# A one-core layer-norm MLP: one transpose group moved, two engines' halves swapped, and the bias turned on another engine

## The chip, the cores and the metric

The kernel runs on one core of a Trainium2 chip. The core has five engines with instruction streams of their own: TensorE (PE in the profile; its weight loads are listed apart as PEld), VectorE (DVE), ScalarE (ACT), GpSimd (POOL) and SyncE (SP). They meet only through semaphores. Transfers between the chip's main memory and the core's own memory are issued by SP and, for the first two of them, by ACT. The metric is the device time of one execution in microseconds (us); lower is better.

## What is computed

```python
def _layernorm(x, axis=-1, eps=1e-5):
    m = jnp.mean(x, axis=axis, keepdims=True)
    v = jnp.var(x, axis=axis, keepdims=True)
    return (x - m) / jnp.sqrt(v + eps)

def reference(x, w1, b1, w2, b2):
    y = _layernorm(x, axis=-1)
    h = _gelu(jnp.einsum("bsd,df->bsf", y, w1) + b1)
    return jnp.einsum("bsf,fd->bsd", h, w2) + b2
```

All arrays are bf16: x is 2048 x 1024, w1 is 1024 x 3584, b1 has 3584 elements, w2 is 3584 x 1024, b2 has 1024. The GELU is the tanh form.

## The kernel before

The 2048 rows of x are 16 tiles of 128 rows, in 4 blocks of 4 tiles. A block is normalised, transposed (so that the 1024 features lie on partitions, 8 slices of 128), multiplied by w1 in 28 output rows of 128 features x 512 columns (8 matmuls each), passed through the GELU with b1 as a bias per partition, and multiplied by w2 in 8 groups of 28 matmuls; DVE adds b2 and SP stores the result. All of w1 and w2 stays in the core's memory.

The program is written as five lists of operations, one for each engine, in the order in which each engine will run them (`_Prog`, `_emit`): an operation names the events that it waits for, and an engine that waits holds all that is queued behind. The order of TensorE is written out by hand for block 0. DVE's later order (scalings of block 0, normalisation and transposes of the next blocks, additions of b2) is merged by estimated times at the end of the function.

Block 0 is the part that the change touches.

- *Loads.* ACT's queue issues the second half of tile 0 (`x0b`, columns 512 to 1023) and then tile 1 (`x1`). SP's queue issues the rest in the order of `SP_FIRST_LOADS`: the first half of tile 0 (`x0a`), six rows of w1 for the first 7 output rows (`w0` to `w5`), the two halves of tile 2, the bias `b1`, two more rows of w1, the halves of tile 3, then wide chunks of w1 (`w8` and on), later blocks of x, and w2. Every transfer is line 190.
- *The head.* Tile 0 is not waited for in full. DVE takes statistics of `x0b` (`op_stats(0, 1)`, line 261) while ACT sums `x0a` with an accumulating copy (line 495, result `half_sb`). DVE joins the two into the row's mean times 4 (`op_mean0`, line 272, event `m4`), and writes tile 0 centred, but not scaled, into `o_sb` in two pieces (line 278): columns 0 to 255, then 256 to 1023. Tile 1 is centred in the same way, in place (line 283). Tiles 2 and 3 are normalised in full (line 287), with 1/sqrt(variance) from POOL (line 265). The missing scale of tiles 0 and 1 is applied by DVE to the sums in PSUM (line 426), after `ops_rbc` has spread the row scales over partitions with 16 small transposes (lines 322 and 330).
- *Transposes of block 0* are TensorE's (`pe_T`, line 376), each group followed by a copy by ACT out of PSUM (line 383). Tile 0 has three groups of slices, 0 to 1, 2 to 4 and 5 to 7 (`GROUPS_0`); the first and the third go to the bank `ps_t`, the second to another. Tiles 1 to 3 have two groups of four, all in `ps_t`; a group waits until ACT has read out the one before it in its bank. Groups are put between the small matmuls (128 columns, line 416) at the indices in `T_PUTS`, counted in the matmuls of block 0's first 7 rows; the first two groups of tile 0 precede them all. Tile 0's third group stands behind 14 matmuls, tile 1's two groups behind 21 and 35.
- *The bias* is loaded as 28 rows of 128 (`b1r_sb`) and transposed by one small TensorE matmul ahead of tile 2's second group (`B1_AT`, line 368) into the free end of that group's bank; a second ACT copy makes the 128 x 28 tile `b1_sb` (line 387), which every GELU (line 433) reads.
- *Warm-up.* 34 matmuls on constants run from the start (line 491), 3 more wait for `m4`, and 3 stand behind the second transpose group.
- *After the first 7 rows* come rows 7 to 27 of block 0 with 512-column matmuls, each waiting for a free PSUM bank: row 7 takes `ps_t`, row 8 the bank of row 0, which its GELU must have read.
- *Constants.* POOL writes `ones`, the identity, `nhalf` and two constant fields of `st_sb` (lines 257 and 258); DVE waits for the last (line 499) before anything else.

Of the kernel before, what the change touches and what calls it, by code (L numbers as in the profile page):

```python
# [20 lines left out]
WARM_A = ((34, None), (3, "m4"))  # L21
WARM_B = 3
N_CENTRED = 2
T_PUTS = {0: (None, None, 14), 1: (21, 35), 2: (96, 118), 3: (140, 156)}
NORM = {0: (0, 2, 8), 1: (0, 4, 8), 2: (0, 4, 8)}
GROUPS_0 = (0, 2, 5, 8)
WAVE_ROWS_0 = 6
WAVE_K = (0, 2, 4, 5, 6, 8)
B1_AT = (2, 1)
GROUPS_1 = (0, 4, 8)  # L30
W1_CHUNK_COLS = (512, 512, 1024, 640)
N_W2_CHUNKS = 4
SP_FIRST_LOADS = ("x0a", "w0", "w1", "w2", "w3", "w4", "w5", "x2a", "x2b", "b1", "w6", "w7", "x3a", "x3b", "w8")
ACT_FIRST_LOADS = ("x0b", "x1")

T_PE_START = 5.7
# [55 lines left out]
def bass_standalone__mixer_channel_mlp__prompt_kernel(  # L92
# [10 lines left out]
    ST, D = xf.shape  # L103
    F = w1.shape[1]
    NT = ST // P
    DT = D // P
    FT = F // P
# [3 lines left out]
    HC = D // 2  # L111
# [34 lines left out]
    with ExitStack() as es:  # L146
# [5 lines left out]
        x_sb = sb("x_sb", [P, NT, D], BF16)  # L152
# [1 line left out]
        hT_sb = sb("hT_sb", [P, FT, TB], BF16)  # L154
        o_sb = sb("o_sb", [P, NOB, D], BF16)
        b2_sb = sb("b2_sb", [P, D], BF16)
        b1r_sb = sb("b1r_sb", [FT, P], BF16)
        b1_sb = sb("b1_sb", [P, FT], F32)
        ident = sb("ident", [P, P], BF16)
        ones = sb("ones", [P, P], BF16)  # L160
# [25 lines left out]
        x_ev = {}  # L186
        w1_issued = set()

        def dma(dst, src, sig, nbytes):
            dma_q[0].op(lambda e, dst=dst, src=src: e.dma_start(dst, src), sig=sig, sem="d_" + sig, inc=16)  # L190
            dma_bytes[0] += nbytes
            est[sig] = DMA_T0 + dma_bytes[0] / DMA_BYTES_PER_US

# [19 lines left out]
        def issue(item):  # L213
            if item[0] == "x" and item[-1] in "ab":
                i, h = int(item[1:-1]), "ab".index(item[-1])
                dma(x_sb[:, i, h * HC:(h + 1) * HC], xf[i * P:(i + 1) * P, h * HC:(h + 1) * HC], f"x{i}_{h}",
                    P * HC * 2)
                x_ev[i] = (f"x{i}_0", f"x{i}_1")
            elif item == "b1":
                dma(b1r_sb[:, :], b1.rearrange("(t p) -> t p", p=P), "b1", F * 2)  # L220
            elif item[0] == "x":
                load_x_tile(int(item[1:]))
            elif item[0] == "w" and int(item[1:]) < len(w1_chunks):
                load_w1(int(item[1:]))
# [7 lines left out]
        for i in range(TPB):  # L232
            if i not in x_ev:
                load_x_tile(i)
            else:
                for h, evn in enumerate(x_ev[i]):
                    if evn not in est:
                        issue(f"x{i}" + "ab"[h])
        if "b1" not in est:
            issue("b1")  # L240
        for ci in range(len(w1_chunks)):
            if ci not in w1_issued:
# [14 lines left out]
        pool.op(lambda e: e.memset(st_sb[:, :, 12:14], 0.0))  # L257
        pool.op(lambda e: e.memset(st_sb[:, :, 14:15], LN_EPS * D), sig="eps")

        def op_stats(i, h):  # L260
            return (lambda e, i=i, h=h: e.bn_stats(st_sb[:, i, 6 * h:6 * (h + 1)], x_sb[:, i, h * HC:(h + 1) * HC]),  # L261
                    [x_ev[i][h]], f"st{i}_{h}", 0.65)
# [6 lines left out]
                    [f"st{i}_0", f"st{i}_1", "eps"], f"mv{i}", 0.33)  # L269

        def op_mean0():
            return (lambda e: e.tensor_scalar(out=m4_sb[:, :], in0=st_sb[:, 0, 7:8], scalar1=st_sb[:, 0, 10:11],  # L272
                                              scalar2=half_sb[:, :], op0=ALU.add, op1=ALU.add),
                    ["st0_1", "half"], "m4", 0.1)

        def op_norm(i, c0, c1, sig):
            if i == 0:
# [16 lines left out]
        def ops_norm(i):  # L294
            cuts = NORM.get(i, (0, DT))
            y_ev[i] = []
            res = []
            for k, (j0, j1) in enumerate(zip(cuts[:-1], cuts[1:])):
                res.append(op_norm(i, j0 * P, j1 * P, f"y{i}_{k}"))
                y_ev[i] += [f"y{i}_{k}"] * (j1 - j0)  # L300
            return res

        def ln_seq(tiles, between):
            seq = []
            prev = None
            for i in tiles:
                for h in range(2):
                    seq.append(op_stats(i, h))
                    if h == 0 and prev is not None:
                        seq += ops_norm(prev)  # L310
                        prev = None
                seq.append(op_aggr(i))
                if i + 1 in between:
                    prev = i
                else:
                    seq += ops_norm(i)
            return seq

        def ops_rbc():
            res = []  # L320
            for i in range(N_CENTRED):
                res.append((lambda e, i=i: e.tensor_scalar(out=rq_sb[:, i, :], in0=ones[:, 0:32],
                                                           scalar1=rstd_sb[:, i:i + 1], scalar2=(1.0 if i else 0.25),
                                                           op0=ALU.mult, op1=ALU.mult),
                            ["ones", f"rstd{i}"], f"rq{i}", 0.1))
            for tq in range(4):
                for q in range(4):
                    src = rq_sb[32 * tq:32 * (tq + 1), :, :]
                    dst = rbc_sb[32 * q:32 * (q + 1), :, 32 * tq:32 * (tq + 1)]
                    res.append((lambda e, src=src, dst=dst: e.transpose(out=dst, in_=src), [f"rq{N_CENTRED - 1}"],  # L330
                                ("rbc" if tq == 3 and q == 3 else None), 0.1))
            return res
# [27 lines left out]
        def pe_T(i, groups, k, with_b1=False):  # L360
            blk, t = divmod(i, TPB)
            j0, j1 = groups[k], groups[k + 1]
            bname, bap = t_banks[k if i == 0 else 0]
            evs = yT_ev.setdefault(i, [None] * DT)
            if with_b1:
                o = (j1 - j0) * P
                b1t = bap[:, o:o + FT]
                pe.op(lambda e: e.transpose(out=b1t, in_=b1r_sb[:, :], identity=ident[0:FT, 0:FT]),  # L368
                      waits=["ident", "b1"] + ([bank_read[bname]] if bname in bank_read else []))
            for j in range(j0, j1):  # L370
                waits = []
                if j == j0:
                    waits = ["ident"] + ([bank_read[bname]] if bname in bank_read else [])
                if j == j0 or y_ev[i][j] != y_ev[i][j - 1]:
                    waits.append(y_ev[i][j])
                pe.op(lambda e, i=i, j=j, o=(j - j0) * P, bap=bap: e.transpose(  # L376
                    out=bap[:, o:o + P], in_=(x_sb[:, i] if i else o_sb[:, 0])[:, j * P:(j + 1) * P],
                    identity=ident[:, :]),
                    waits=waits, sig=(f"tp{i}_{k}" if j == j1 - 1 else None))
# [3 lines left out]
            act.op(lambda e, dst=dst, src=src: e.copy(out=dst, in_=src), waits=[f"tp{i}_{k}"], sig=f"te{i}_{k}")  # L383
            bank_read[bname] = f"te{i}_{k}"
            if with_b1:
                bank_read[bname] = "b1c"
                act.op(lambda e: e.copy(out=b1_sb[:, :], in_=b1t), waits=[f"tp{i}_{k}"], sig="b1c")
            pe_t[0] += (j1 - j0) * 0.056

        crit = []  # L390
# [98 lines left out]
        def warm(n, gate=None):  # L489
            for _ in range(n):  # L490
# [4 lines left out]
        act.op(lambda e: e.activation(out=o_sb[:, 1, 0:HC], in_=x_sb[:, 0, 0:HC], func=ACT.Copy, scale=2.0 / HC,  # L495
                                      accum_out=half_sb[:, :]), waits=[x_ev[0][0]], sig="half")
        for n, gate in WARM_A:
            warm(n, gate)
        dve.op(None, waits=["eps"])
        head = [op_stats(0, 1), op_mean0()] + ops_norm(0) + ln_seq([1], ()) + [op_stats(0, 0), op_aggr(0)]  # L500
        for o in head + ln_seq(list(range(2, TPB)), ()) + ops_rbc():
            dve_put(o)

        for k in range(2):
# [19 lines left out]
            order.insert(n, ("T", t, k))  # L524
        for c in order:
            if c[0] == "T":
                pe_T(c[1], GROUPS_1 if c[1] else GROUPS_0, c[2], with_b1=(c[1:] == B1_AT))
# [102 lines left out]
```

## Time and profile before

| | us |
|---|---|
| median of 3 runs | 398.64 |
| lowest and highest run | 398.64 and 398.94 |
| profiled execution, its own time | 398.81 |
| profiled execution, span from first to last instruction | 397.5 |

The granted TensorE clock was 1.000 in the profiled execution. A row of a timeline gives the start of a group of instructions and its length in us, engine, line, operation, what is written from what, the shape and the count; in brackets stands the engine's idle time just before and what ended it. Groups of one engine can overlap, since an instruction's record runs until its result is written, while the next has already started. A row of the chain gives start, length and what it was. A row of the transfers ends with the size of one and the us from issue to landing.

### The profile page before, as it was taken

The page shows a single profiled execution, that of the slowest core. Times are in us where ns is not written, and L with a number is a line of the kernel's source. Part 1 is how long each engine was busy: PE and PEld are TensorE (multiplying, and loading weights), DVE is VectorE, ACT ScalarE, POOL GpSimd, SP SyncE. Part 2 cuts the span into 40 slices and gives each one's busy share as a digit, 9 for nine tenths or more (in the row PEclk, how much of TensorE's full clock was granted, in tenths as well). Part 3 has the DMA queues.
Part 4 walks back from the last instruction along what each step waited for, and adds up shares of the span by engine and source line. Part 5 has one row for each costly group of instructions (what it writes and reads, how often), then busy time and mean ns, then how long its engine had stood idle before and what let it go on. Part 6 is the DMA issues. An engine that isn't in the chain of part 4 may idle for free.

```text
span 397.5 us, 4880 instructions
## 1 busy us (share of the span) xinstructions
PE 394.0 (99%) x2117; PEld 191.4 (48%) x2117; DVE 152.8 (38%) x341; ACT 83.0 (21%) x125; POOL 9.8 (2%) x25
## 2 busy tenths in 40 slices
PE   8999999999999999999999999999999999999998
PEld 7954444444444444444444444444444444444447
DVE  5837899989999005988100000001100000001011
ACT  4364330000134432000024434100003334400000
POOL 2101000020001000000000000000000000000000
DMA  8999930000000000000000000000000000000000
GB/s 288 359 378 386 387 136 13 26 29 13 27 2 0 2 0 0 29 13 26 28 13 0 2 0 2 11 16 28 13 26 15 0 0 2 0 13 28 13 28 26
DMA packets 16798, 23.64 MB, mean 59 GB/s; under 512 B 1546, under 2 KB 10378, under 8 KB 16778
## 3 DMA queue, kind: packets, MB, share of 16 engines
q1 hardware_dynamic: 16490, 22.95, 16.4%
q10 hardware_dynamic: 288, 0.39, 0.3%
q8 instruction: 16, 0.26, 0.3%
q14 instruction: 4, 0.03, 0.0%
HBM read 19.14 MB, written 4.19 MB: 59 GB/s over the span
## 4 chain that ended last, share of the span: by engine, by line
PE 98%; DMA 1%; DVE 0%; ACT 0%; issue 0%; DVEq 0%
PE ps L467 49%; PE ps L416 41%; PE ps_t L416 8%; DMA x_sb<-in_x_dram 1%; PE ps_t L376 1%; DVE st_sb L261 0%; PE ps L491 0%; ACT yT_sb L383 0%; PE ps L376 0%; DVE o_sb L478 0%; DVE m_sb L272 0%; PE ps_t L368 0%; DVEq L79 0%
## 5 line engine op out<-in xcount | busy, mean ns | idle before, releaser
L467 PE MATMUL ps<-w_sb,hT_sb 128*128 128x512 bf16 (+1 forms) x980 | 194.2, 361 | 0.0
L416 PE MATMUL ps<-yT_sb,w_sb 128*128 128x512 bf16 (+1 forms) x920 | 167.3, 340 | 0.1
L467 PEld LDWEIGHTS ps<-w_sb,hT_sb 128*128 128x128 bf16 x980 | 91.3, 98 | 102.6
L416 PEld LDWEIGHTS ps<-yT_sb,w_sb 128*128 128x128 bf16 x920 | 80.9, 98 | 82.3 <-issue 0.2
L433 ACT ACTIVATE hT_sb<-ps,b_sb 128x512 bf16<-128x512 f32 x94 | 63.9, 688 | 236.6 <-PE ps L416 217.1
L478 DVE TENSOR_TENSOR o_sb<-ps,b_sb 128x512 bf16<-128x512 f32 (+1 forms) x35 | 22.6, 646 | 198.2 <-PE ps L467 198.1
L348 DVE STREAM_TRANSPOSE yT_sb<-x_sb 32x256 bf16<-32x256 bf16 x192 | 83.7, 436 | 26.6 <-PE ps_t L416 23.5
L416 PE MATMUL ps_t<-yT_sb,w_sb 128*128 128x512 bf16 x144 | 34.0, 379 | 0.0
L261 DVE BATCH_NORM_STATS2 st_sb<-x_sb 128x6 f32<-128x512 bf16 x32 | 21.1, 673 | 4.3 <-DMA x_sb<-in_x_dram 4.2
L416 PEld LDWEIGHTS ps_t<-yT_sb,w_sb 128*128 128x128 bf16 x144 | 14.1, 98 | 16.7
L433 ACT ACTIVATE hT_sb<-ps_t,b_sb 128x512 bf16<-128x512 f32 x18 | 12.4, 689 | 17.4 <-PE ps_t L416 14.5
L426 DVE TENSOR_TENSOR ps<-ps,rbc_sb 128x256 f32<-128x256 f32 x24 | 9.7, 428 | 7.0 <-PE ps L416 6.7
L265 POOL TENSOR_TENSOR rstd_sb<-mv_sb,nhalf 128x1 f32<-128x1 f32 x16 | 8.9, 559 | 119.2 <-DVE mv_sb L268 119.2
L287 DVE TENSOR_SCALAR x_sb<-x_sb,mv_sb,rstd_sb 128x1024 bf16<-128x1024 bf16 (+1 forms) x15 | 7.8, 525 | 3.9 <-POOL rstd_sb L265 3.3
L383 ACT COPY yT_sb<-ps_t 128x512 bf16<-128x512 bf16 (+2 forms) x8 | 4.4, 545 | 8.6 <-PE ps_t L376 8.6
L491 PE MATMUL ps<-const-bfloat16-1.0 128*128 128x128 bf16 x40 | 4.0, 278 | 1.4 <-PEq L615 0.8
L491 PEld LDWEIGHTS ps<-const-bfloat16-1.0 128*128 128x128 bf16 x40 | 3.6, 129 | 1.5 <-issue 0.8
L268 DVE BATCH_NORM_AGGREGATE mv_sb<-st_sb 128x2 f32<-128x15 f32 x16 | 3.5, 221 | 1.3
L330 DVE STREAM_TRANSPOSE rbc_sb<-rq_sb 32x64 f32<-32x64 f32 x16 | 3.8, 236 | 0.2
L376 PE MATMUL ps_t<-ident,x_sb 128*128 128x128 bf16 x24 | 2.4, 220 | 0.2 <-ACT yT_sb L383 0.2
L426 DVE TENSOR_TENSOR ps_t<-ps_t,rbc_sb 128x256 f32<-128x256 f32 x4 | 1.6, 410 | 1.7 <-PE ps_t L416 1.7
L376 PEld LDWEIGHTS ps_t<-ident,x_sb 128*128 128x128 bf16 x24 | 1.5, 98 | 0.4 <-ACT yT_sb L383 0.4
(24 smaller groups left out, 7.6 us busy)
## 6 DMA issues: line engine op xcount, KB each, us to landing
w_sb<-in_w_dram SPq DMA_DIRECT2D x4, 1792.0 KB, 18.1
out_dram<-o_sb SPq DMA_DIRECT2D x31, 128.0 KB, 1.7
x_sb<-in_x_dram SPq DMA_DIRECT2D x3, 1024.0 KB, 14.0
w_sb<-in_w_dram SPq DMA_DIRECT2D x2, 1024.0 KB, 9.6
w_sb<-in_w_dram SPq DMA_DIRECT2D x1, 2048.0 KB, 15.1
w_sb<-in_w_dram SPq DMA_DIRECT2D x8, 224.0 KB, 4.2
w_sb<-in_w_dram SPq DMA_DIRECT2D x1, 1280.0 KB, 15.4
x_sb<-in_x_dram SPq DMA_DIRECT2D x5, 128.0 KB, 4.2
```

The lines of the kernel that those rows point to most:

```text
L261: return (lambda e, i=i, h=h: e.bn_stats(st_sb[:, i, 6 * h:6 * (h + 1)], x_sb[:, i, h * HC:(h + 1) * HC]), [x_ev[i][h]], f"st{i}_{h}", 0.65)
L265: pool.op(lambda e, i=i: e.tensor_tensor(out=rstd_sb[:, i:i + 1], in0=mv_sb[:, i, 1:2], in1=nhalf[:, i:i + 1], op=ALU.pow), waits=[f"mv{i} ...
L287: return (lambda e, i=i, c0=c0, c1=c1: e.tensor_scalar(out=x_sb[:, i, c0:c1], in0=x_sb[:, i, c0:c1], scalar1=mv_sb[:, i, 0:1], scalar2=rst ...
L348: res.append((lambda e, src=src, dst=dst: e.transpose(out=dst, in_=src), waits, (f"tr{i}" if lastop else None), 0.47))
L376: pe.op(lambda e, i=i, j=j, o=(j - j0) * P, bap=bap: e.transpose(out=bap[:, o:o + P], in_=(x_sb[:, i] if i else o_sb[:, 0])[:, j * P:(j + ...
L383: act.op(lambda e, dst=dst, src=src: e.copy(out=dst, in_=src), waits=[f"tp{i}_{k}"], sig=f"te{i}_{k}")
L416: pe.op(lambda e, b=b, r=r, dt=dt, n0=n0, n1=n1, bank=bank: e.matmul(unit_bank(bank)[:, n0:n1], lhsT=w1_sb[:, dt, r * P:(r + 1) * P], rhs= ...
L426: crit.append((est[wait_ev], (lambda e, ap=ap: e.tensor_tensor(out=ap, in0=ap, in1=rbc_sb[:, :, :].rearrange("p t s -> p (t s)"), op=ALU.m ...
L433: act.op(lambda e, r=r, n0=n0, n1=n1, bank=bank: e.activation(out=hT_sb[:, r, n0:n1], in_=unit_bank(bank)[:, n0:n1], func=ACT.Gelu_apprx_tanh,
L467: pe.op(lambda e, st=st, ft=ft, c0=c0, c1=c1, bank=bank: e.matmul(ps_2[:, bank, 0:c1 - c0], lhsT=hT_sb[:, ft, st * P:(st + 1) * P], rhs=w2 ...
L478: crit.append((est[sig], (lambda e, ob=ob, c0=c0, c1=c1, bank=bank: e.tensor_tensor(out=o_sb[:, ob, c0:c1], in0=ps_2[:, bank, 0:c1 - c0], ...
L491: pe.op(lambda e: e.matmul(ps_1[:, 0, 0:P], lhsT=unit, rhs=unit, start=True, stop=True), waits=[gate] if gate else [])
```

## The change

Six edits, all of block 0's start:

1. Tile 0's third transpose group stands behind 6 matmuls, not 14.
2. DVE takes its statistics of `x0a` and ACT sums `x0b`.
3. The two constant fields of `st_sb` are written by DVE, and its wait for POOL falls away; POOL writes zeros into the new bias tile instead.
4. The bias is loaded in four strips: strip q holds, on partitions 32q to 32q+27, the 32 elements that belong to partitions 32q to 32q+31 of the result. The strips wait for POOL's zeros.
5. The bias stands behind the halves of tile 3 in SP's order, not behind those of tile 2.
6. The bias is transposed in 32 x 32 blocks and widened to f32 by DVE, between the normalisation of tile 3 and the spreading of the row scales; TensorE's transpose and ACT's copy of it are gone.

```diff
-T_PUTS = {0: (None, None, 14), 1: (21, 35), 2: (96, 118), 3: (140, 156)}
+T_PUTS = {0: (None, None, 6), 1: (21, 35), 2: (96, 118), 3: (140, 156)}
...
-SP_FIRST_LOADS = ("x0a", "w0", "w1", "w2", "w3", "w4", "w5", "x2a", "x2b", "b1", "w6", "w7", "x3a", "x3b", "w8")
+SP_FIRST_LOADS = ("x0a", "w0", "w1", "w2", "w3", "w4", "w5", "x2a", "x2b", "w6", "w7", "x3a", "x3b", "b1", "w8")
...
-        b1r_sb = sb("b1r_sb", [FT, P], BF16)
+        b1r_sb = sb("b1r_sb", [P, 32], BF16)
+        b1t_sb = sb("b1t_sb", [P, 32], BF16)
...
-                dma(b1r_sb[:, :], b1.rearrange("(t p) -> t p", p=P), "b1", F * 2)
+                b1v = b1.rearrange("(t q a) -> q t a", q=4, a=32)
+                for q in range(4):
+                    dma(b1r_sb[32 * q:32 * q + FT, :], b1v[q], f"b1{q}", F // 2, waits=["b1z"])
...
-        pool.op(lambda e: e.memset(st_sb[:, :, 12:14], 0.0))
-        pool.op(lambda e: e.memset(st_sb[:, :, 14:15], LN_EPS * D), sig="eps")
+        pool.op(lambda e: e.memset(b1r_sb[:, :], 0.0), sig="b1z")
+        dve.op(lambda e: e.memset(st_sb[:, :, 12:14], 0.0))
+        dve.op(lambda e: e.memset(st_sb[:, :, 14:15], LN_EPS * D), sig="eps")
...
-            return (lambda e: e.tensor_scalar(out=m4_sb[:, :], in0=st_sb[:, 0, 7:8], scalar1=st_sb[:, 0, 10:11],
+            return (lambda e: e.tensor_scalar(out=m4_sb[:, :], in0=st_sb[:, 0, 1:2], scalar1=st_sb[:, 0, 4:5],
                                               scalar2=half_sb[:, :], op0=ALU.add, op1=ALU.add),
-                    ["st0_1", "half"], "m4", 0.1)
+                    ["st0_0", "half"], "m4", 0.1)
...
+        def ops_b1():
+            return [(lambda e: e.transpose(out=b1t_sb[:, :], in_=b1r_sb[:, :]), [f"b1{q}" for q in range(4)], "b1t", 0.2),
+                    (lambda e: e.tensor_copy(b1_sb[:, :], b1t_sb[:, 0:FT]), ["b1t"], "b1c", 0.1)]
...
-            if with_b1:
-                o = (j1 - j0) * P
-                b1t = bap[:, o:o + FT]
-                pe.op(lambda e: e.transpose(out=b1t, in_=b1r_sb[:, :], identity=ident[0:FT, 0:FT]),
-                      waits=["ident", "b1"] + ([bank_read[bname]] if bname in bank_read else []))
...
-            if with_b1:
-                bank_read[bname] = "b1c"
-                act.op(lambda e: e.copy(out=b1_sb[:, :], in_=b1t), waits=[f"tp{i}_{k}"], sig="b1c")
...
-        act.op(lambda e: e.activation(out=o_sb[:, 1, 0:HC], in_=x_sb[:, 0, 0:HC], func=ACT.Copy, scale=2.0 / HC,
-                                      accum_out=half_sb[:, :]), waits=[x_ev[0][0]], sig="half")
+        act.op(lambda e: e.activation(out=o_sb[:, 1, 0:HC], in_=x_sb[:, 0, HC:D], func=ACT.Copy, scale=2.0 / HC,
+                                      accum_out=half_sb[:, :]), waits=[x_ev[0][1]], sig="half")
...
-        dve.op(None, waits=["eps"])
-        head = [op_stats(0, 1), op_mean0()] + ops_norm(0) + ln_seq([1], ()) + [op_stats(0, 0), op_aggr(0)]
-        for o in head + ln_seq(list(range(2, TPB)), ()) + ops_rbc():
+        head = [op_stats(0, 0), op_mean0()] + ops_norm(0) + ln_seq([1], ()) + [op_stats(0, 1), op_aggr(0)]
+        for o in head + ln_seq(list(range(2, TPB)), ()) + ops_b1() + ops_rbc():
             dve_put(o)
```

More of the change, by code (lines that the diff above doesn't have):

```diff
@@ L28 @@
 WAVE_K = (0, 2, 4, 5, 6, 8)
-B1_AT = (2, 1)
 GROUPS_1 = (0, 4, 8)
@@ L187, in bass_standalone__mixer_channel_mlp__prompt_kernel, with dma @@
         w1_issued = set()
-        def dma(dst, src, sig, nbytes):
-            dma_q[0].op(lambda e, dst=dst, src=src: e.dma_start(dst, src), sig=sig, sem="d_" + sig, inc=16)
+        def dma(dst, src, sig, nbytes, waits=()):
+            dma_q[0].op(lambda e, dst=dst, src=src: e.dma_start(dst, src), waits=waits, sig=sig, sem="d_" + sig, inc=16)
             dma_bytes[0] += nbytes
@@ L238, in bass_standalone__mixer_channel_mlp__prompt_kernel @@
                         issue(f"x{i}" + "ab"[h])
-        if "b1" not in est:
+        if "b10" not in est:
             issue("b1")
@@ L358, in bass_standalone__mixer_channel_mlp__prompt_kernel, with pe_T @@
         t_banks = [("t", ps_t[:, 0, :]), ("2_0", ps_2b[:, 0, :]), ("t", ps_t[:, 0, :])]
-        def pe_T(i, groups, k, with_b1=False):
+        def pe_T(i, groups, k):
             blk, t = divmod(i, TPB)
@@ L526, in bass_standalone__mixer_channel_mlp__prompt_kernel @@
             if c[0] == "T":
-                pe_T(c[1], GROUPS_1 if c[1] else GROUPS_0, c[2], with_b1=(c[1:] == B1_AT))
+                pe_T(c[1], GROUPS_1 if c[1] else GROUPS_0, c[2])
             else:
```

## The prediction

> **What bounds the kernel now.** I read the page's busy shares and the shares of the chain that ended last, then that chain in order of time over the first 40 us, then the timeline of each engine over the first 24 us, and last the landing times of the first transfers.
>
> ```profile
> span 397.5 us, 4880 instructions
> PE 394.0 (99%) x2117; PEld 191.4 (48%) x2117; DVE 152.8 (38%) x341; ACT 83.0 (21%) x125; POOL 9.8 (2%) x25
> PE 98%; DMA 1%; DVE 0%; ACT 0%; issue 0%; DVEq 0%
> ```
>
> TensorE is busy 99% of the span and is 98% of the chain. From the first layer's matmuls on it hardly waits, so whatever starts it earlier, or takes an instruction out of its stream, moves the end by as much; nothing on another engine counts unless it makes TensorE wait. The change can only act in the first 20 us. There the chain in order of time has these links that are not matmuls:
>
> ```profile
> 0.78 2.80 DMA x_sb<-in_x_dram
> 3.68 0.70 DVE st_sb L261
> 4.41 0.28 DVE m_sb L272
> ...
> 7.13 0.49 ACT yT_sb L383
> 7.61 0.05 issue
> ```
>
> Up to 4.69 us the end hangs on a half tile of x that lands at 3.58, DVE's statistics of it, and the mean. Later comes one excursion: tile 0's third group is transposed, ACT copies it out (7.13 to 7.61), and only 0.05 us behind that may tile 1's first group start, since both use the bank ps_t. TensorE's own timeline gives the pace and the two places that change:
>
> ```profile
> 5.98 0.94 PE L416 MATMUL ps<-yT_sb,w_sb 128*128 128x128 bf16 x14
> 6.76 0.33 PE L376 MATMUL ps_t<-ident,o_sb 128*128 128x128 bf16 x3
> 6.93 0.55 PE L416 MATMUL ps<-yT_sb,w_sb 128*128 128x128 bf16 x7
> 7.66 0.40 PE L376 MATMUL ps_t<-ident,x_sb 128*128 128x128 bf16 x4 [0.18 <-ACT yT_sb L383]
> ...
> 8.97 3.57 PE L416 MATMUL ps<-yT_sb,w_sb 128*128 128x128 bf16 x61
> 12.38 0.39 PE L376 MATMUL ps_t<-ident,x_sb 128*128 128x128 bf16 x4
> 12.60 1.39 PE L416 MATMUL ps<-yT_sb,w_sb 128*128 128x128 bf16 x22
> 13.92 0.18 PE L368 MATMUL ps_t<-ident,b1r_sb 28*128 28x28 bf16 x1
> 14.04 0.40 PE L376 MATMUL ps_t<-ident,x_sb 128*128 128x128 bf16 x4
> ```
>
> Durations here overlap, so pace comes from starts: 61 matmuls from 8.97 to 12.38 are 0.0559 us each; 14 from 5.98 to 6.76 agree.
>
> **The third group, eight matmuls sooner.** The 7 matmuls from 6.93 would let the next instruction start at 6.93 + 7 x 0.0559 = 7.32; it starts at 7.66. The hole is 0.34 us, of which the row calls 0.18 idle (the rest is the modelled tail of the last matmul). After the change the order is 6 matmuls, 3 transposes, 15 matmuls. The transposes start at 5.98 + 6 x 0.0559 = 6.32, so ACT's copy, 0.37 us behind their start as now (6.76 to 7.13), runs 6.69 to 7.17 and frees the bank at 7.22. TensorE comes to tile 1's group at 6.32 + 0.17 + 15 x 0.0559 = 7.33: the copy is covered, with 0.11 us to spare. What else could hold it:
>
> ```profile
> 5.46 0.37 ACT L383 COPY yT_sb<-ps_t 128x256 bf16<-128x256 bf16 x1 [1.31 <-PE ps_t L376]
> 5.77 0.48 ACT L383 COPY yT_sb<-ps 128x384 bf16<-128x384 bf16 x1
> 6.89 0.35 DVE L283 TENSOR_SCALAR x_sb<-x_sb,mv_sb 128x512 bf16<-128x512 bf16 x1
> ```
>
> The moved group's bank was read out by 5.83 and its normalised columns are those that the second group already waits for, so it waits for nothing new; ACT is done with the second group at 6.25. Late next is DVE's first half of tile 1: it ends at 7.24, with the same 0.05 us of signal 7.29, 0.04 us ahead of TensorE, thin but enough. I take 0.33 us of gain; the bounds are 0.18 (the row's idle time) and 0.34 (the whole hole). Tile 1's second group waits for the copy of its first as now; both move together.
>
> **The bias off TensorE.** Without the 28x28 transpose, tile 2's second group could start at 12.60 + 22 x 0.0559 = 13.83 and starts at 14.04. Gain 0.21 us; the lower bound is the step from 13.92 to 14.04, 0.12. ACT's small cast goes too; it lay beside TensorE's matmuls and is worth nothing.
>
> **What DVE gets instead.** A transpose and a copy of 28 columns, ahead of the broadcast of the row scales, and the constants at the start:
>
> ```profile
> 1.34 0.13 POOL L257 MEMSET st_sb<- 128x32 f32 x1
> 14.16 0.38 DVE L322 TENSOR_SCALAR rq_sb<-ones,rstd_sb 128x32 f32<-128x32 bf16 x2
> 14.57 3.98 DVE L330 STREAM_TRANSPOSE rbc_sb<-rq_sb 32x64 f32<-32x64 f32 x16
> 18.83 2.44 DVE L426 TENSOR_TENSOR ps<-ps,rbc_sb 128x256 f32<-128x256 f32 x7 [0.27 <-PE ps L416]
> 19.30 4.15 ACT L433 ACTIVATE hT_sb<-ps,b_sb 128x512 bf16<-128x512 f32 x7 [1.67 <-DVE ps L426]
> 22.36 1.89 PE L416 MATMUL ps<-yT_sb,w_sb 128*128 128x512 bf16 x8
> ```
>
> No row has the two bias operations; by the nearest, the 32x64 transposes (3.98/16 = 0.25) and the 128x32 scalings (0.2 from one to the next), they are about 0.45 us together, bounds 0.3 and 0.8 (for two as slow as the two scalings together). The broadcast then ends at 19.0 instead of 18.55 and the first scaling starts at about 19.05, not 18.83; the first GELU starts 0.47 behind it as now and ends 0.6 (4.15/7) later, near 20.1. Who waits: TensorE wants that bank for row 8, at 22.36 less 0.54, so 21.8. There is 1.7 us of cover, more at each later row (GELU 0.6 apart, rows longer). Cost nothing. The constants cost nothing either: 0.13 us each on POOL, in a time when DVE waits for its first data until 3.68.
>
> **The queue.** Five issues of SP from the bias to the first wide chunk of weights take 7.35 - 5.04, 0.46 us each. Taking the bias out from behind tile 2 puts two weight rows and tile 3 forward by 0.46 us; four strips instead of one transfer put the wide chunk back by 3 x 0.46 = 1.4 us:
>
> ```profile
> 5.04 0.46 SPq L190 DMA_DIRECT2D b1r_sb<-in_b_dram  x1
> 7.35 0.43 SPq L190 DMA_DIRECT2D w_sb<-in_w_dram  x1
> w_sb<-in_w_dram SPq DMA_DIRECT2D x1, 1024.0 KB, 8.3
> x_sb<-in_x_dram SPq DMA_DIRECT2D x2, 128.0 KB, 4.1
> 20.64 1.89 PE L416 MATMUL ps_t<-yT_sb,w_sb 128*128 128x512 bf16 x8
> ```
>
> That chunk lands at 7.35 + 8.3 = 15.7 and is wanted at 20.64: 5 us of margin, 1.4 lost at most. The strips are issued at about 6.9, 7.3, 7.8 and 8.3; at the 4.1 us of their neighbours from tile 3 the last lands near 12.4, 1.8 us before DVE asks at 14.2. Their wait is for a memset of POOL in the first 2 us, long over when SP gets there.
>
> **The halves swapped.** DVE now reads the half from SP's queue, ACT the one from its own; they land 2.6 and 2.8 us behind their issues:
>
> ```profile
> x_sb<-in_x_dram ACTq DMA_DIRECT2D x1, 128.0 KB, 2.8
> x_sb<-in_x_dram SPq DMA_DIRECT2D x1, 128.0 KB, 2.6
> 0.79 0.38 SPq L190 DMA_DIRECT2D x_sb<-in_x_dram  x1
> 3.43 0.63 ACT L495 ACTIVATE o_sb<-x_sb 128x512 bf16<-128x512 bf16 x1 [0.45 <-DMA x_sb<-in_x_dram]
> 3.96 0.19 ACT L495 ACTIVATION_READ_ACCUMULATOR o_sb<-x_sb 128x1 f32 x1
> ```
>
> The mean needs both. ACT's part takes 0.72 us (3.43 to 4.15), DVE's 0.70. On the early half (3.39) DVE ends near 4.19; on the late one (3.58) ACT starts 0.04 to 0.10 behind the landing (as ACT does at 3.43 and DVE at 3.68) and ends at 4.34 to 4.40, and its result reaches DVE 0.03 to 0.10 later: mean at 4.37 to 4.50, against 4.41. The other half sets the end now and I take 0; bounds 0.04 gained and 0.09 lost if the landings stay, 0.25 gained (3.68 less 3.43) if ACT's half comes as early as SP's.
>
> **Sum.** 0.33 + 0.21 + 0 = 0.54 us off a span of 397.5: 396.96. The profiled execution took 398.81 us, 1.31 more than its span, and lies 0.17 above the median of the runs, 398.64; less 0.54 that is 398.10. The bounds add up to 0.18 + 0.12 - 0.09 = 0.21 and 0.34 + 0.21 + 0.25 = 0.80 of gain.
>
> **Rivals.** *The head is shortened too*: ACT's half lands as early as SP's, and the mean comes 0.25 us sooner: 397.85. For it: the two transfers are issued within 0.01 us of each other. Against it: nothing in the change touches them.
>
> *The holes close in part*: tile 1's first group waits for DVE, whose margin is 0.04 us, or only the 0.12 us step falls away with the bias, or the mean is 0.09 us late: 0.18 + 0.12 = 0.30 of gain, 0.21 with the mean late as well: about 398.4. For it: that margin. Against it: DVE's chain moves with the mean, so a late head opens no new hole.
>
> *The strips come late* (slower): if the four went one after the other, each with the shortest landing time shown, 2.6 us, the last would land at 6.9 + 4 x 2.6 = 17.3. DVE stands there with all that is queued behind it: the broadcast ends 0.45 + 4.39 later (4.39 is 14.16 to 18.55), at 22.1, and the first GELU 0.05 + 0.47 + 0.6 after that, at 23.2, where TensorE wants its bank at 21.8. It waits 1.4 us: 398.10 + 1.4 = 399.5. It decides from a landing at 15.9 on. Against it, the weight rows at the start of the queue:
>
> ```profile
> w_sb<-in_w_dram SPq DMA_DIRECT2D x2, 224.0 KB, 3.8
> w_sb<-in_w_dram SPq DMA_DIRECT2D x2, 224.0 KB, 4.4
> ```
>
> The first and the last pair of six, issued half a microsecond apart, land 3.8 and 4.4 us behind their issue, so landing times run side by side on this queue. The Trainium skill speaks for the rival: "DMA: Bandwidth & Descriptors", section "Rules for kernel authors", has small transfers joined into one large one, since under 64 KB nearly all is overhead. By these two rows that overhead is latency that overlaps; this trace holds no landing of a transfer as small as a strip to test it on.
>
> **How the numbers follow.** A measurement of this kernel tells about 0.2% from no change, 0.8 us: 397.84 to 399.44 is no change. Forecast 0.58 (398.10; its own range 397.8 to 398.4, by the spread of 0.30 in the three runs); head shortened too 0.12 (397.85, half of it inside the 0.2%); holes closed in part 0.18 (398.4); strips late 0.07 (399.5); 0.05 is left for something slower that I don't see. Faster 0.08, within 0.80, slower 0.12. The range goes from 397.6, the short head less most of a spread, to 398.9, the partly closed holes with a spread and 0.2 more; late strips stay outside.
>
> **What would show it.** Tile 1's first group starts 0.33 us earlier than 7.66, with no idle time charged to ACT; 22 matmuls and tile 2's second group follow each other without the 0.21; the mean starts within 0.1 us of 4.41, released by ACT instead of DVE; the first scaling starts at about 19.05, behind DVE's own broadcast; row 7 starts at about 20.1. The forecast is wrong if the mean starts 0.2 us or more away from 4.41, if DVE waits for the strips, or if TensorE waits for a GELU.

## The result and the profile after

| | before | changed |
|---|---|---|
| median of 22 runs each, us | 398.99 | 398.39 |
| lowest and highest run, us | 398.64 to 399.63 | 398.14 to 398.65 |
| profiled execution, its own time, us | 398.81 | 398.20 |
| its span, us | 397.5 | 396.9 |

The ratio is 0.9986 with a 95% interval from 0.998 to 0.9992: 0.14% faster, 0.56 us (0.32 to 0.80), clear of zero but inside the 0.2% that the prediction calls no change. The medians differ by 0.60 us and the spans by 0.6. The page of the changed kernel, its head and the shares of the chain that ended last:

```profile
span 396.9 us, 4883 instructions
PE 394.1 (99%) x2116; PEld 191.7 (48%) x2116; DVE 152.8 (38%) x345; ACT 82.8 (21%) x124; POOL 9.7 (2%) x24
PE 99%; ACT 0%; DVE 0%; issue 0%
```

There is one instruction less on TensorE. The transfer of x is gone from the chain, which now runs through the warm-up matmuls; TensorE still waits for the mean, since the weight load of the three matmuls behind it stands 0.24 us for DVE, until 4.58. TensorE's timeline of the changed kernel:

```profile
5.92 0.49 PE L415 MATMUL ps<-yT_sb,w_sb 128*128 128x128 bf16 x6
6.25 0.33 PE L378 MATMUL ps_t<-ident,o_sb 128*128 128x128 bf16 x3
6.42 1.00 PE L415 MATMUL ps<-yT_sb,w_sb 128*128 128x128 bf16 x15
7.25 0.39 PE L378 MATMUL ps_t<-ident,x_sb 128*128 128x128 bf16 x4
...
11.96 0.39 PE L378 MATMUL ps_t<-ident,x_sb 128*128 128x128 bf16 x4
...
13.41 0.39 PE L378 MATMUL ps_t<-ident,x_sb 128*128 128x128 bf16 x4
...
20.00 1.89 PE L415 MATMUL ps_t<-yT_sb,w_sb 128*128 128x512 bf16 x8
```

Two distances carry the gain. From the first matmul of the first layer to tile 1's first group: 7.25 - 5.92 = 1.33 us, where it was 7.66 - 5.98 = 1.68, so 0.35 less, with no idle time left on the row. From tile 2's first group to its second: 13.41 - 11.96 = 1.45, where it was 14.04 - 12.38 = 1.66, so 0.21 less. The first matmul itself starts 0.06 earlier, and row 7 at 20.00 instead of 20.64. The first distance flatters the change. Counted from the mean, which releases all that follows, the first matmul came later than before (5.92 - 4.25 = 1.67 us behind it, against 5.98 - 4.41 = 1.57), and tile 1's group came at 7.25 - 4.25 = 3.00 instead of 7.66 - 4.41 = 3.25: 0.25 less, not 0.35. The 0.10 is a slow start of TensorE in this execution, which the last section comes to. DVE in the same stretch:

```profile
4.25 0.27 DVE L275 TENSOR_SCALAR m_sb<-st_sb,half_sb 128x1 f32<-128x1 f32 x1 [0.31 <-ACT o_sb L494]
...
6.73 0.35 DVE L286 TENSOR_SCALAR x_sb<-x_sb,mv_sb 128x512 bf16<-128x512 bf16 x1
...
14.54 0.20 DVE L323 STREAM_TRANSPOSE b1t_sb<-b1r_sb 128x32 bf16<-128x32 bf16 x1
...
14.87 0.38 DVE L329 TENSOR_SCALAR rq_sb<-ones,rstd_sb 128x32 f32<-128x32 bf16 x2
...
19.37 2.42 DVE L425 TENSOR_TENSOR ps<-ps,rbc_sb 128x256 f32<-128x256 f32 x7
```

The mean is now released by ACT, 0.31 us after DVE was free for it. The bias costs DVE 0.33 us (14.54 to 14.87), and the first scaling no longer waits for TensorE but for DVE's own broadcast. The two half tiles with their landing times in us at the end of the row, and ACT's first copy:

```profile
x_sb<-in_x_dram ACTq DMA_DIRECT2D x1, 128.0 KB, 2.6
x_sb<-in_x_dram SPq DMA_DIRECT2D x1, 128.0 KB, 2.4
```
```profile
5.40 0.37 ACT L385 COPY yT_sb<-ps_t 128x256 bf16<-128x256 bf16 x1 [1.26 <-PE ps_t L378]
```

Both halves (2.8 and 2.6 before) landed 0.2 us earlier in this execution than in the profile before, which puts the mean forward from 4.41 to about 4.22; it starts at 4.25. Whether that belongs to the change is what the experiments had to say.

### The profile page after: what moved, and what is told of

It is laid out like the page before. It is cut to its first block, busy times and chain, and to the rows that moved or that the text cites. A ratio compares the mean times of both kernels' runs of the same rounds, so it can differ in the third digit from the quotient of the medians.

```text
span 396.9 us, 4883 instructions
## 1 busy us (share of the span) xinstructions
PE 394.1 (99%) x2116; PEld 191.7 (48%) x2116; DVE 152.8 (38%) x345; ACT 82.8 (21%) x124; POOL 9.7 (2%) x24
## 4 chain that ended last, share of the span: by engine, by line
PE 99%; ACT 0%; DVE 0%; issue 0%
PE ps L466 49%; PE ps L415 41%; PE ps_t L415 8%; PE ps L490 1%; PE ps_t L378 0%; ACT yT_sb L385 0%; DVE o_sb L477 0%
```

## The experiments

My theory was the prediction's: two holes in TensorE's stream are closed, and the head (landing, statistics, mean) is worth nothing. The rival was that the swap of the halves made the mean earlier. The times of all runs, each against runs of the kernel before on the same chip:

| run | median, us | before, us | ratio | 95% interval |
|---|---|---|---|---|
| e1, moved group only | 398.60 | 398.90 | 0.9994 | 0.9985 to 1.0003 |
| e2, bias edits only | 398.62 | 398.90 | 0.9992 | 0.9983 to 1.0001 |
| e3, swap only | 399.10 | 398.90 | 1.0003 | 0.9994 to 1.0012 |
| e4, group behind 10 matmuls | 398.41 | 398.90 | 0.9989 | 0.9980 to 0.9998 |
| e5, strips late | 402.68 | 398.83 | 1.0102 | 1.0070 to 1.0134 |
| e7, more work on DVE | 398.37 | 398.83 | 0.9990 | 0.9981 to 0.9999 |
| e8, order of the wave | 398.37 | 398.83 | 0.9988 | 0.9979 to 0.9997 |
| e9, early wait for weights | 398.42 | 398.83 | 0.9990 | 0.9981 to 0.9999 |
| e10, three edits of the head | 398.33 | 398.98 | 0.9986 | 0.9977 to 0.9994 |
| e11, changed kernel again | 398.49 | 398.98 | 0.9986 | 0.9978 to 0.9995 |
| e12, halves swapped back | 398.38 | 398.98 | 0.9987 | 0.9978 to 0.9996 |

The ratio is not exactly the quotient of the two medians. The intervals are about 0.09% wide to each side, 0.36 us (0.32% in e5), so single terms of 0.1 to 0.3 us are read from the distances in the traces, and the times only have to agree.

**e1, the moved group alone**, in the kernel before:

```diff
-T_PUTS = {0: (None, None, 14), 1: (21, 35), 2: (96, 118), 3: (140, 156)}
+T_PUTS = {0: (None, None, 6), 1: (21, 35), 2: (96, 118), 3: (140, 156)}
```

> The kernel before with one edit: tile 0's third transpose group behind 6 matmuls instead of 14. Theory (the change's gain is two holes in TensorE's stream closed): 0.33 us faster than before, about 0.08%, and tile 1's first group starts within 0.05 us of 1.34 us behind the first matmul of the first layer (6 x 0.0559 + 0.17 + 15 x 0.0559) where it was 7.66 - 5.98 = 1.68 behind it; the step to the bias transpose ahead of tile 2's second group stays. Rival (the gain is the head, because the mean started at 4.25 instead of 4.41 in the profile of the changed kernel): no change of the time here, and the hole opens again behind another wait.

TensorE's and DVE's timelines of e1, and the weight load of tile 1's first group:

```profile
5.87 0.49 PE L416 MATMUL ps<-yT_sb,w_sb 128*128 128x128 bf16 x6
...
6.36 1.00 PE L416 MATMUL ps<-yT_sb,w_sb 128*128 128x128 bf16 x15
7.28 0.38 PE L376 MATMUL ps_t<-ident,x_sb 128*128 128x128 bf16 x4
```
```profile
6.78 0.62 DVE L283 TENSOR_SCALAR x_sb<-x_sb,mv_sb 128x512 bf16<-128x512 bf16 x2
```
```profile
7.25 0.24 PEld L376 LDWEIGHTS ps_t<-ident,x_sb 128*128 128x128 bf16 x4
```

The distance is 7.28 - 5.87 = 1.41: 0.27 of the 1.68 - 1.34 = 0.34 us. A hole of 7.28 - 6.36 - 15 x 0.0559 = 0.08 us is left, and ACT's copy is not in it. DVE's first half of tile 1, 0.35 us long, ends at 7.13; TensorE's weight load follows 0.12 behind that and the matmul 0.15, where the prediction had taken 0.05 for this signal. So its "thin" margin of 0.04 was not enough. The median moved by 0.30 us, in line, but the interval holds no change.

**e2, the bias edits alone.** The changed kernel with the group back behind 14 matmuls and DVE and ACT on their former halves:

```diff
-T_PUTS = {0: (None, None, 6), 1: (21, 35), 2: (96, 118), 3: (140, 156)}
+T_PUTS = {0: (None, None, 14), 1: (21, 35), 2: (96, 118), 3: (140, 156)}
...
-        head = [op_stats(0, 0), op_mean0()] + ops_norm(0) + ln_seq([1], ()) + [op_stats(0, 1), op_aggr(0)]
+        head = [op_stats(0, 1), op_mean0()] + ops_norm(0) + ln_seq([1], ()) + [op_stats(0, 0), op_aggr(0)]
```

> The changed kernel with the third group back behind 14 matmuls and the halves swapped back, so that the bias edits (strips, their place in the queue, the constants, the transpose by DVE) stand alone. Theory: 0.21 us faster than before (0.05%), with 22 matmuls between tile 2's two groups followed by the second at 1.45 us (0.22 + 22 x 0.0559) behind the first's start, where it was 14.04 - 12.38 = 1.66; the 0.34 us hole ahead of tile 1's first group is there. Rival (the head): no change. Rival (the longer way over DVE costs something): slower than 0.21 faster by what TensorE waits for a GELU, which the profile would show as idle time at row 8.

TensorE's timeline and the chain in order of time, of e2:

```profile
12.37 0.39 PE L378 MATMUL ps_t<-ident,x_sb 128*128 128x128 bf16 x4
12.60 1.39 PE L415 MATMUL ps<-yT_sb,w_sb 128*128 128x128 bf16 x22
13.83 0.39 PE L378 MATMUL ps_t<-ident,x_sb 128*128 128x128 bf16 x4
```
```profile
0.78 2.88 DMA x_sb<-in_x_dram
3.66 0.02 issue
3.68 0.70 DVE st_sb L264
4.39 0.03 issue
4.41 0.28 DVE m_sb L275
```

The distance is 1.46 (1.45 forecast), and the time is 0.28 us less, in line, though its interval too holds no change. The hole ahead of tile 1's first group is still there, at 7.66 as before. The chain shows one thing that nobody had priced: the later half lands at 3.66 and DVE starts at 3.68. In the profile before it started 0.10 behind a landing at 3.58. Since DVE writes its own constants, its wait for POOL in front of the wait for x is gone, and that wait cost 0.08 us although POOL had been done since 1.52.

**e3, the swap alone**, in the kernel before (DVE's order, the fields of the mean and ACT's half, as in the change):

```diff
-        head = [op_stats(0, 1), op_mean0()] + ops_norm(0) + ln_seq([1], ()) + [op_stats(0, 0), op_aggr(0)]
+        head = [op_stats(0, 0), op_mean0()] + ops_norm(0) + ln_seq([1], ()) + [op_stats(0, 1), op_aggr(0)]
```

> The kernel before with the halves swapped and nothing else. Theory: no change (within 0.1 us); the mean starts 0.87 us behind the landing of the later half, released by ACT, where it started 0.83 behind it before (3.58 to 4.41), so at worst 0.04 us later at equal landings. Rival (the swap shortens the head, which is where the change's time came from): 0.16 to 0.25 us faster, with the mean 0.6 us or less behind the landing of the half that ACT reads.

The chain of e3 in order of time:

```profile
0.78 2.64 DMA x_sb<-in_x_dram
...
3.44 0.73 ACT o_sb L495 x2
...
4.27 0.28 DVE m_sb L272
```

The mean starts 0.85 us behind the landing at 3.42 (it was 0.83 before), behind ACT's sum and not DVE's statistics. The time shows no gain; its median is 0.2 us higher, inside its interval. The rival falls: the early mean of the changed kernel's profile came with early landings, and e4, which has the swap too, started its mean at 4.40. What is not settled is whether the swap moves the landings themselves: the later half lands between 3.38 and 3.53 in the eight kept traces with the swap and between 3.47 and 3.72 in the five without. The two overlap, and neither e3 nor e12 shows a gain in time from the swap.

**e4, the group behind 10 matmuls**, in the changed kernel:

```diff
-T_PUTS = {0: (None, None, 6), 1: (21, 35), 2: (96, 118), 3: (140, 156)}
+T_PUTS = {0: (None, None, 10), 1: (21, 35), 2: (96, 118), 3: (140, 156)}
```

> The changed kernel with the third group behind 10 matmuls instead of 6. Theory: the bank is free 0.37 + 0.48 + 0.05 = 0.90 us behind the group's start, and TensorE comes to tile 1's first group 0.17 + 11 x 0.0559 = 0.78 behind it: a hole of 0.12 us, so 0.12 us slower than the changed kernel and 0.42 faster than before. Rival (the place of the group doesn't matter once it is off 14): as fast as the changed kernel, 0.56 us faster than before, no hole.

TensorE's timeline of e4, and ACT's copy of the third group:

```profile
6.52 0.33 PE L378 MATMUL ps_t<-ident,o_sb 128*128 128x128 bf16 x3
6.69 0.78 PE L415 MATMUL ps<-yT_sb,w_sb 128*128 128x128 bf16 x11
7.42 0.40 PE L378 MATMUL ps_t<-ident,x_sb 128*128 128x128 bf16 x4
```
```profile
6.89 0.48 ACT L385 COPY yT_sb<-ps_t 128x384 bf16<-128x384 bf16 x1 [0.65 <-PE ps_t L378]
```

From the third group to tile 1's first it is 7.42 - 6.52 = 0.90 us, exactly the copy's round trip (0.37 to its start, 0.48 for it, 0.05 behind it), where the 3 transposes and 11 matmuls take 0.78: the hole of 0.12 is there, and the trace confirms the theory and its size. The time cannot: 0.11% (0.44 us) less than before, with 0.36 us of interval to each side, it holds both the 0.42 of the theory and the 0.56 of the rival. Behind tile 1's first group a second hole of 0.14 us opened in e4, at a weight row that landed at 8.14.

**e5, the strips late**, in the changed kernel:

```diff
-SP_FIRST_LOADS = ("x0a", "w0", "w1", "w2", "w3", "w4", "w5", "x2a", "x2b", "w6", "w7", "x3a", "x3b", "b1", "w8")
+SP_FIRST_LOADS = ("x0a", "w0", "w1", "w2", "w3", "w4", "w5", "x2a", "x2b", "w6", "w7", "x3a", "x3b", "w8", "w9", "b1")
```

> The changed kernel with the four strips issued behind two wide chunks of weights instead of ahead of them. Theory (a strip lands in the order of its queue; TensorE waits only for what goes beyond the cover): the second chunk lands near 18 us (18.6 in the profile before), DVE's bias transpose starts then instead of at 14.54, 3.5 us later; the first scaling follows 4.83 behind it (14.54 to 19.37) and the first GELU ends 1.07 behind that, near 24, where row 8 wants its bank at 21.73: about 2.2 us slower than the changed kernel, some 400.6. Rival (small transfers are served beside the large ones, 4 to 5 us behind their issue near 8.5): they land by 13.5, DVE doesn't wait, no change.

DVE and TensorE in e5:

```profile
18.92 0.21 DVE L323 STREAM_TRANSPOSE b1t_sb<-b1r_sb 128x32 bf16<-128x32 bf16 x1 [4.51 <-DMA b1r_sb<-in_b_dram]
```
```profile
20.39 1.89 PE L415 MATMUL ps_t<-yT_sb,w_sb 128*128 128x512 bf16 x8
24.97 8.81 PE L415 MATMUL ps<-yT_sb,w_sb 128*128 128x512 bf16 x40 [2.69 <-ACT hT_sb L432]
```

This is the prediction's slower rival, made to happen. The strips land in the order of their queue at about 18.9, DVE stands for 4.51 us, and TensorE waits at row 8 for the first GELU: 24.97 instead of 20.39 + 1.73 = 22.12, 2.85 us. So in this execution a landing from 18.9 - 2.85 = 16.05 on decides; the prediction said 15.9. The span grew by 3.3 us: the stall, and 0.39 by which row 7 started later than in the changed kernel's profile (20.39 against 20.00), for the most part from a slow start of TensorE. The four runs took 401.41, 401.55, 403.81 and 404.78 us, so the median in the table lies between two pairs. The first two, of which the profiled one is the first, had a granted clock of 1.000 and are the stall; the last two had 0.996 and 0.992, which over 400 us is 1.6 and 3.2 us, most of the 2.3 and 3.3 us by which they are longer. The Trainium skill ("TensorE: Matmul & The Clock Gate", section "Part 1: The HAM clock gate") says that an idle window of about 3.4 us puts TensorE back to half clock. The profiled run agrees, with 2.69 us idle and full pace behind it (40 matmuls in 8.81 us, 8.80 in e7, which had no such stall); no trace was taken of the two runs with the lower clock, so that their stall crossed the window is not shown.

**e7, sixteen more transposes on DVE**, in the changed kernel, ahead of the bias and into a spare tile:

```diff
+        def ops_b1_more(n):
+            return [(lambda e, k=k: e.transpose(out=b1x_sb[:, k, :], in_=b1r_sb[:, :]), [f"b1{q}" for q in range(4)], None, 0.2)
+                    for k in range(n)]
...
-        for o in head + ln_seq(list(range(2, TPB)), ()) + ops_b1() + ops_rbc():
+        for o in head + ln_seq(list(range(2, TPB)), ()) + ops_b1_more(16) + ops_b1() + ops_rbc():
```

> The changed kernel with 16 more transposes of the bias strips, into a spare tile, ahead of the one that counts. Theory: DVE's longer way is hidden up to a cover of 1.3 us (first GELU's end at 19.84 + 0.6 against row 8 at 21.73); 16 transposes of 0.1 to 0.2 us add 1.6 to 3.2 us, so row 8 starts later by that less 1.3, 0.3 to 1.9 us, and the time grows by the same. Rival (the bias work on DVE is not covered, part of its 0.45 us was paid already): the time grows by all of what is added. Rival (later banks are what counts): no change.

DVE and TensorE in e7:

```profile
14.11 1.60 DVE L328 STREAM_TRANSPOSE b1x_sb<-b1r_sb 128x32 bf16<-128x32 bf16 x16
15.64 0.17 DVE L324 STREAM_TRANSPOSE b1t_sb<-b1r_sb 128x32 bf16<-128x32 bf16 x1
```
```profile
20.18 1.89 PE L420 MATMUL ps_t<-yT_sb,w_sb 128*128 128x512 bf16 x8
21.91 8.80 PE L420 MATMUL ps<-yT_sb,w_sb 128*128 128x512 bf16 x40
```

The transposes are 0.096 us apart and add 1.53 us. Row 8 follows row 7 by the usual 1.73, and the time is that of the changed kernel. I had expected a stall of 0.3 us or more; DVE came to the bias 0.43 us earlier here than in the changed kernel's profile (14.11 against 14.54, with tile 2's transfer) and TensorE to row 8 0.18 later (21.91 against 21.73), and the cover was that much larger. In the changed kernel's profile it is 21.73 - 19.84 - 0.6 = 1.29 us, so there 1.53 us more would have stalled TensorE by an estimated 0.24. The rival that part of DVE's bias work is paid falls: 1.53 us more of it cost nothing. The third rival, that later banks decide, also has no change and is not told apart by this run; e5's stall at row 8 speaks against it.

**e8, another order of the wave**, in the changed kernel:

```diff
-T_PUTS = {0: (None, None, 6), 1: (21, 35), 2: (96, 118), 3: (140, 156)}
+T_PUTS = {0: (None, None, 6), 1: (24, 42), 2: (96, 118), 3: (140, 156)}
...
-WAVE_K = (0, 2, 4, 5, 6, 8)
+WAVE_K = (0, 2, 4, 6, 6, 8)
```

> The changed kernel with a slice of tile 0 (7 matmuls) moved ahead of tile 1's first matmuls, and tile 1's two groups behind 24 and 42 matmuls instead of 21 and 35. Theory (what holds tile 1's first group now is DVE's normalisation, 0.07 us in the run with the group alone, and its second group the copy of the first, 0.06 us): both holes close, 0.06 to 0.13 us faster than the changed kernel; below what the time can tell, but the starts show it: 61 + 35 matmuls and two groups without a hole. Rival (the weight rows hold TensorE at this place, as in the run with the group behind 10, where the fifth row landed at 3.11 + 5.0 = 8.11): no gain, holes ahead of the fifth or sixth slice instead.

TensorE's matmuls, its weight loads and DVE in e8:

```profile
6.37 1.35 PE L415 MATMUL ps<-yT_sb,w_sb 128*128 128x128 bf16 x18
7.71 0.38 PE L378 MATMUL ps_t<-ident,x_sb 128*128 128x128 bf16 x4
```
```profile
7.38 0.17 PEld L415 LDWEIGHTS ps<-yT_sb,w_sb 128*128 128x128 bf16 x3 [0.18 <-DMA w_sb<-in_w_dram]
```
```profile
5.56 1.29 DVE L264 BATCH_NORM_STATS2 st_sb<-x_sb 128x6 f32<-128x512 bf16 x2 [0.33 <-DMA x_sb<-in_x_dram]
```

18 matmuls are 1.01 us and tile 1's group starts 1.34 behind their first: a hole of 0.33, in two parts. For about half of it TensorE waited for a weight row, as the rival had it, though at an earlier slice. For the rest it waited for DVE, which had stood 0.33 us for tile 1's transfer, so that its normalisation was late again. The time shows no gain; what the run shows is that landings of the first transfers, which differ by some tenths of a us between executions, now reach TensorE.

**e9, the wait for the first weight row put ahead**, in the changed kernel:

```diff
-        warm(WARM_B)
+        warm(WARM_B, "w1c0")
```

> The changed kernel with the wait for the first weight row put on the three warm-up matmuls behind the second transpose group. Theory (the 0.12 us from the end of ACT's first copy to the first weight load of the first layer, against 0.05 at tile 1's first group, is a second wait that the sequencer takes up behind the first): the step shrinks to about 0.05 us, 0.07 us gained. Rival (the step is the time of the copy's signal and of the matmuls queued ahead): unchanged at 0.12 us.

The weight loads of the first layer's first matmuls, in the changed kernel and in e9:

```profile
5.89 0.18 PEld L415 LDWEIGHTS ps<-yT_sb,w_sb 128*128 128x128 bf16 x3 [0.29 <-issue]
```
```profile
5.82 0.17 PEld L415 LDWEIGHTS ps<-yT_sb,w_sb 128*128 128x128 bf16 x2
```

ACT's copy ends at 5.77 in the changed kernel (5.40 + 0.37) and at 5.76 in e9. The step shrinks from 0.12 to 0.06 us, as expected. The time doesn't show it.

**e10, e11 and e12: the head's waits.** e12 swaps the halves back in the changed kernel; e10 also has e9's edit and, at tile 1's first group, DVE's event ahead of the bank's; e11 is the changed kernel.

```diff
-                    waits.append(y_ev[i][j])
+                    waits.insert(0, y_ev[i][j]) if i == 1 and j == 0 else waits.append(y_ev[i][j])
```

> The changed kernel with three edits: the halves swapped back, the wait for the first weight row on the warm-up matmuls, and at tile 1's first group the wait for DVE ahead of the one for the bank. Theory (an event that comes late in the second of two waits costs 0.05 to 0.08 us more than in the only or the first one): the mean starts 0.75 us behind the later half's landing, as in the run with the bias edits alone, not 0.87; the first layer's first weight load 0.06 behind ACT's copy, as in the run before, not 0.12; tile 1's first group 0.05 behind DVE's first half of tile 1, not 0.12. Together 0.17 to 0.24 us less than the changed kernel, some 0.75 less than before (0.19%), if no weight row comes late. Rival (the landings of the first transfers decide in most executions): as the changed kernel, 0.5 less than before.

> The changed kernel itself, beside the two others on one chip. Both theories: 0.9986 of before within 0.0010; the mean 0.85 to 0.87 us behind the later half's landing.

> The changed kernel with the halves swapped back and nothing else. Theory (the swap takes away nothing and puts the late event behind a second wait): the mean 0.75 us behind the later half's landing, 0.1 us less than the changed kernel. Rival (the swap is what lets the mean start early): the mean 0.85 or more behind it, 0 to 0.2 us more than the changed kernel.

The chain of e10 in order of time, and DVE's first half of tile 1 with TensorE's weight load behind it:

```profile
0.78 2.94 DMA x_sb<-in_x_dram
...
4.48 0.28 DVE m_sb L275
```
```profile
6.96 0.35 DVE L286 TENSOR_SCALAR x_sb<-x_sb,mv_sb 128x512 bf16<-128x512 bf16 x1
```
```profile
7.36 0.23 PEld L378 LDWEIGHTS ps_t<-ident,x_sb 128*128 128x128 bf16 x4
```

All three distances came out: the mean 4.48 - 3.72 = 0.76 us behind the landing, the group's weight load 0.05 behind DVE's end at 7.31, and the first layer's 0.05 behind ACT's copy. The mean stands 0.86 us behind the later landing in e11 and 0.75 in e12, as both had it. In time e10 is 0.65 us below before and e11 0.49, a difference of 0.16 in the forecast's direction that the intervals don't separate. So e10 has the lowest median on this chip, and is not shown to beat the changed kernel. e12 is 0.11 below e11, equally open; in its profiled execution tile 1's transfer came late, DVE stood 0.17 us for it, and TensorE lost 0.24 us ahead of tile 1's first group (7.49 instead of 7.25).

## Why the prediction was right

- *Third group sooner, 0.33 us.* Right in cause and nearly in size. e1 gave 0.27 in the trace and 0.30 in the median; in the changed kernel's own profile it was 0.25 counted from the mean. e4's hole of 0.12 us is the copy's round trip at work. What was named as late next, DVE's first half of tile 1, was indeed it. The term that was too small is its signal, taken as 0.05 us like the bank's: in e1 the matmul started 0.15 behind DVE's end, and 0.04 to spare became a hole of 0.08. In the changed kernel's profile the hole is absent because TensorE's slow start gave DVE 0.10 us more: without it TensorE would have come to the group at an estimated 7.15, against 7.08 + 0.15 = 7.23 for DVE.
- *Bias off TensorE, 0.21 us.* Right: 0.20 in e2, 0.21 in the changed kernel.
- *DVE's longer way, nothing.* Right, though the room was smaller than said: 0.33 us of work instead of 0.45, but DVE came to it at 14.54 instead of 14.16, and the cover was 1.29 us instead of 1.7. The rival with late strips was to decide from a landing at 15.9 on; e5 gives 16.05, in an execution whose row 7 was 0.39 later.
- *The queue, nothing.* Right. The strips were there when DVE asked. The wide chunk's issue went back, at 8.70, by 8.70 - 7.35 = 1.35 us without reaching TensorE.
- *The constants on DVE, nothing.* Right for the whole change, wrong for the edit alone. In e2 dropping DVE's wait for POOL gains 0.08 us at the head (0.10 to 0.02). With the swap, ACT's sum releases the mean and nothing of this is left: the mean is 0.86 us behind the landing with the constants on DVE (e11) and 0.85 with them on POOL (e3).
- *The swap, 0 between -0.04 and +0.09.* Right within its bounds: the mean comes 0.85 to 0.87 us behind the landing instead of 0.83, because ACT's event comes late and behind another wait. Without the swap the changed kernel has 0.75 (e2, e10, e12), so the swap costs about 0.1 us. ACT's half did not land as early as SP's, as the rival with a short head had it: issued together, they landed 2.6 and 2.4 us later.
- *Sum, 398.10 us.* The span of 396.96 was measured as 396.9, which is partly luck: of the 0.64 us by which row 7 came sooner, 0.16 is the early landing of x in this execution, and the two holes gave 0.25 + 0.21 = 0.46 (0.27 + 0.20 in e1 and e2) where 0.54 was forecast. The median is 398.39 and not 398.10 mainly because the 3 runs shown for before had a median 0.35 us below that of 22. The difference, 0.54 forecast, is 0.56 by the ratio, whose interval of 0.32 to 0.80 holds 0.46 as well. Of the signs listed, the early landing put two off: the mean started 0.16 from 4.41, not within 0.1, and tile 1's first group 0.41 earlier, not 0.33. The first scaling came at 19.37, not 19.05.

## What to carry to other kernels

Where one engine is 98% of the chain, look for holes in its own stream: take the pace from the starts of a long run of equal instructions, extrapolate to the next one, and ask which event it waited for; the idle time on the row (0.18 us here) is only part of the hole (0.34). When a hand-over closes, the next late event is a few hundredths of a us away, and transfers whose landing varies by tenths begin to matter. Gains of this size are read from distances inside one trace, not from the times, and the distance has to start at the event that releases the whole stretch (here the mean): from the first matmul on it was 0.10 us too good.

## What the runs showed that was not expected

*A second wait has a price even when its event is long past.* An instruction with two waits, of which the one that is late stands last, started 0.10 to 0.12 us behind the late event; alone or ahead of the other it took 0.02 to 0.06. It was seen at DVE's statistics (0.10 before, 0.02 in e2), at the first layer's first weight load (0.12, 0.06 in e9) and at tile 1's first group (0.12 in e1, where DVE ended at 7.13 and the weight load started at 7.25; 0.05 in e10). In the changed kernel's profile the third place shows nothing, since TensorE's own stream came to the group no earlier. The chain of the kernel before shows what stands between the landing at 3.58 and DVE's statistics at 3.68:

```profile
3.61 0.02 DVEq L79
3.63 0.05 issue
```

Line 79 is where the program emits a wait. A second wait has become an instruction of its own on DVE's sequencer, and it runs only when the late event is there. The chain of e2, with one wait, has no such row.

*TensorE's start-up pace differs between executions.* In e11, the changed kernel again, the first six matmuls of the first layer were slow; its timeline, and the row of that stretch with the granted clock in the column ahead of the last two:

```profile
5.91 0.80 PE L415 MATMUL ps<-yT_sb,w_sb 128*128 128x128 bf16 x6
6.50 0.40 PE L378 MATMUL ps_t<-ident,o_sb 128*128 128x128 bf16 x3
```
```profile
5.90:6.50 0.60, 0.60 (x8) 0.60 (x7) 0.50 (x2) 0.34 (x1) 0.00 (x0) 1.00 1.03 394
```

Six matmuls take 0.59 us, 0.098 each, where the changed kernel's own profile has 0.33 for the six. From the first matmul to tile 1's group e11 has 7.58 - 5.91 = 1.67 us, as much as the kernel before, although no wait is in it: the 0.26 us that the six took longer hide most of the closed hole.

It is not e11 alone. The six took 0.59 us in e5, 0.51 in e7 and 0.45 in e9, and 0.33 or 0.34 in e1, e8, e10 and e12. By the starts in the kept traces, TensorE's 128-column matmuls are 0.107 us apart at first and turn to 0.056 to 0.060 at some moment: at 3.55 us in the kernel before, at 4.1 in e1 and e2, at 5.3 in the changed kernel, and at 6.6 to 6.7 in e11 and e5. In the changed kernel's profile it was late enough to slow the transposes ahead of the first layer, which is the 0.10 us between the mean and the first matmul. The column says 1.00 for e11 because that trace holds no record of the clock at the start; the traces of e4, the changed kernel and e12 hold one, of the full clock from 5.04, 5.34 and 5.90 us on, and in each the pace turns there. The Trainium skill ("TensorE: Matmul & The Clock Gate", section "Part 1: The HAM clock gate") has matmuls of 128 columns at 107 ns before the clock is released and 56 ns after, with a window that runs free of the kernel's start. The two paces agree with it, and an equal kernel that reaches full pace at different times fits a free window. Whether the change itself has a part in the later turns is not shown: the three traces without its bias edits turn by 4.6 us, of the ten with them three by 4.8 and seven from 5.0 on.
